# Head transposes on TensorE instead of the DMA crossbar, low fp16 halves also on GpSimd, gated products 1024 columns wide, and a new order of steps

## The chip, the cores and the metric

The kernel runs on one core of a Trainium2 chip. The metric is the device time of one execution in microseconds. The core has TensorE (PE, matrix products; its weight loads are listed apart as PEld), VectorE (DVE), ScalarE (ACT), GpSimd (POOL) and SyncE (SP), which here only issues DMAs. Sixteen DMA engines serve all queues. PE writes to eight PSUM banks of 128 x 512 fp32 each; GpSimd does not touch PSUM in this kernel.

## What is computed

The reference is a gated linear recurrence with a complex decay, followed by a gated feed-forward network (FFN):

```
mag = sqrt(a_re**2 + a_im**2);  a = (a_re + i a_im) * min(mag, 0.999) / (mag + 1e-6)
for t in range(768):                      # S: 48 x 48, complex, one per batch and head
    S = a[t][:, None] * S + outer(k[t], v[t])
    y[t] = q[t] @ real(S)
x = y, heads joined: 3072 tokens x 384
out = (sigmoid(x @ w_gate) * (x @ w_val)) @ w_out      # 384 -> 1536 -> 384
```

There are 4 batches, 8 heads and 768 time steps; inputs and output are fp32.

## The kernel before

Time is cut into 6 chunks of 128 steps. A **slab** is one chunk of one batch with its 8 heads: 24 slabs, `m = 0..23`, in 8 groups (`SIZES`) of 2 or 4. Two slabs make a **pair**, the unit of the FFN.

For each group the decays become sums over time: `sq` and `add` make the squared magnitude, `lna`, `lnm` take logarithms, `inv`, `r` and `atan` give the angle. From group 2 on (`SPLIT`) a logarithm or angle is split into two fp16 halves, so that its running sum is two fp16 matmuls instead of an fp32 one. The high half is `lh` (logarithm) or `th` (angle, in turns). The low half is `ll` (lines 630 to 633) or `tl` (lines 767 to 770), one DVE instruction each: clamp or scale the fp32 value, subtract the high half. PE then forms the running sums (`cl` at line 662, `ct` at line 783). ACT takes exponentials (`ee`) and, after DVE has found whole turns (`r16`, line 798) and PE has taken them off (`nid`, line 805), cosines and sines (`cs`).

For each slab `qke` multiplies q and k by the exponentials. `qs` (line 851, DVE) multiplies by cosine and sine and writes a `slot`: 128 time steps x 16 blocks of 128 columns, eight for k and eight for q. Scores need these blocks with time along the columns, so all 16 must be transposed. Slabs 0 to 5 do it on PE: a step `tp` for each half of the heads makes 8 transposes into one PSUM bank (lines 892 and 893), and a step `qkT` copies 128x1024 fp16 values to SBUF (line 521 on DVE or 519 on ACT, in the helper `copied`). Slabs 6 to 23 (`CROSSED`) do it with two DMAs each, `xk` and `xq` (line 871), through the crossbar of the DMA engines, issued on SP's queue between the loads, the small row copies (line 678) and the stores.

Then, for each slab: scores (`sc`, line 911, PE), a causal mask (`mst`, line 926, DVE, two of 128x512), the state of the recurrence (`u`, `x16`, `kv`, `P`), the result `y` (lines 984 and 986), its scaling to fp16 (`y16`), a PE transpose (`xp`, line 1018) and a copy (`xt`) into the FFN's input.

The FFN of a pair has 12 blocks of 128 hidden columns, taken two at a time (`fp = 0..5`): `pg` and `pv` (line 1043, 6 matmuls of 128x256 each) write a bank each, `tanh` (line 1054, ACT) reads the gate's bank and writes `g16`, and `p` (line 1061, DVE) computes (tanh + 1) * value into `p`, 128x512 at a time. `po` (line 1082) multiplies by `w_out`, `ot` scales and `st` (line 1104) stores.

The order is written out. `TIMES` gives each step a due time; `Plan.order` sorts all steps by it, `manual_schedule` emits them in that order, and each engine and each DMA queue works through its own steps in that order. `HOME` names the engine of each movable step (v for DVE, a for ACT, g for GpSimd). `SLOTS` gives each step its buffer or PSUM bank, and `WARM` puts dummy matmuls ahead of some PE steps.

Of the kernel before, what the change touches and what calls it, by code (L numbers as in the profile page):

```python
# [10 lines left out]
ALU = mybir.AluOpType  # L11
# [16 lines left out]
CROSSED = range(6, 24)  # L28
# [6 lines left out]
    "sq": "vagvaaggaagagagaaggagggg",  # L35
    "add": "vvvvgggggggggggggggggggg",
    "lh": "gvggggvggggg",
    "r": "vvgggggggggg",
    "v16": "vavagaggggagggggagavaaga",
    "qke": "vvvggggvggggggggggggvggg",  # L40
    "th": "aagvaagvgaav",
    "ab": "vvavvavaavaaaaaaaaaavaaa",
    "qkT": "vavavvvvavvvvvvvvvvvvvvvvvvvvvvvvvvvvvvvvvvvvvvv",
    "P": "vava",
    "u": "ggggggvggggggggggvgg",
    "x16": "ggaavgaggggvggag",
    "y16": "avvvaavvavavvvavaaavaaaa",
    "xt": "vvvvvvavvvvvavvavvvvvaav",
    "ot": "vvvvvaaavvvvavvaaavvaaavv",
# [4 lines left out]
        27.89, 36.02, 27.27],  # L54
    "wv": [
        31.35, 38.17, 36.03],
    "wo": [
        53.47, 54.3, 65.03],
    "lr": [
        0.75, 2.68, 7.03, 7.06, 24.34, 27.88, 25.83, 26.32, 45.89, 58.15,  # L60
        53.31, 52.18, 71.46, 92.9, 87.25, 85.33, 106.38, 121.07, 118.57,
        112.93, 170.37, 176.96, 133.38, 160.02],
    "la": [
        2.22, 1.85, 10.78, 7.07, 24.5, 26.36, 25.84, 27.87, 48.76, 56.39,
        53.93, 53.32, 75.86, 92.85, 87.77, 85.34, 111.4, 121.08, 121.86,
        118.56, 176.57, 178.21, 153.22, 134.91],
    "sq": [
        7.04, 7.02, 11.86, 9.9, 24.95, 29.54, 26.34, 29.5, 49.21, 58.89,
        56.85, 62.71, 83.72, 96.51, 92.96, 86.01, 112.9, 129.56, 128.24,
        118.61, 180.83, 185.55, 167.29, 170.36],  # L70
    "add": [
        7.05, 7.9, 13.4, 13.88, 26.35, 38.15, 28.5, 38.12, 53.3, 65, 62,
        65.86, 87.2, 96.54, 96.47, 92.92, 121.81, 129.58, 128.25, 129.55,
        184.23, 185.57, 169.56, 170.39],
    "lna": [
        9.92, 14.99, 33.31, 67.86, 98.47, 139.01, 185.56, 171.42],
    "lh": [
        8.54, 14.47, 40.53, 42.65, 69.29, 75.89, 102.61, 103.34, 136.22,
        141.84, 185.59, 172.91],
    "lnm": [  # L80
        11.87, 15.39, 38.16, 66.46, 100.65, 132.15, 185.58, 170.4],
    "inv": [
        9.93, 16.37, 36.01, 70.07, 103.36, 139.02, 186.18, 172.85],
    "r": [
        10.77, 19.16, 40.52, 39.65, 73.59, 75.88, 108.19, 107.9, 142.65,
        142.64, 189.11, 173.82],
    "cl": [
        14.97, 14.96, 17.84, 16.27, 45.44, 42.85, 47.17, 46.54, 70.89, 76.95,
        80.11, 77.54, 104.14, 104.52, 114.2, 116.75, 138.97, 140.17, 148.32,
        149.93, 187.16, 186.78, 181.01, 173.23],  # L90
    "ee": [
        16.91, 14.98, 18.49, 17.83, 47.18, 44.65, 48.42, 47.56, 72.96, 79.27,
        86.25, 79.29, 106.53, 106.39, 114.78, 117.62, 140.01, 141.81, 149.19,
        152.85, 189.76, 189.77, 182.5, 173.81],
    "scr": [
        35.3, 38.13, 41.19, 37.26, 52.64, 53.49, 54.34, 53.48, 87.94, 92.86,
        95.76, 92.91, 118.58, 111.43, 121.83, 124.54, 153.21, 155.22, 160.22,
        160.21, 195.89, 195.1, 187.57, 187.58],
    "rbt": [
        46.92, 48.74, 55.48, 96.46, 126.03, 161.47, 198.36, 188.29],  # L100
    "arr": [
        50.09, 50.04, 55.92, 98.24, 127.86, 161.92, 205.03, 188.88],
    "lk": [
        16.93, 15.41, 15.42, 17.85, 30.76, 49.23, 53.94, 66.48, 75.91, 85.35,
        94.86, 88.08, 112.25, 92.84, 112.27, 118.55, 125.19, 156.21, 161.95,
        146.39, 185.54, 190.51, 161.93, 181.02],
    "lq": [
        16.94, 16.28, 16.95, 21.91, 41.18, 50.73, 62.72, 69.68, 79.24, 92.87,
        95.78, 88.09, 112.26, 104.92, 122.21, 118.59, 155.19, 156.9, 161.96,
        146.4, 190.31, 197.73, 161.94, 190.12],  # L110
    "lv": [
        15.4, 29.55, 9.91, 26.79, 30.86, 50.74, 71.28, 66.47, 52.19, 92.94,
        76.96, 95.79, 133.17, 121.82, 125.2, 146.64, 160.01, 154.52, 171.41,
        166.24, 140.93, 180.62, 192.37, 195.11],
    "v16": [
        15.89, 30.3, 14.95, 27.29, 45.52, 60.69, 71.29, 84.58, 87.19, 101.96,
        114.07, 118.91, 136.26, 130.58, 142.92, 147.37, 164.44, 155.21,
        178.63, 169.53, 167.28, 202.72, 198.62, 205.05],
    "qke": [
        17.82, 16.36, 20.04, 24.35, 48.73, 53.28, 67.87, 71.45, 84.59, 93.48,  # L120
        96.49, 92.93, 112.96, 108.55, 134.93, 121.8, 157.53, 160.03, 167.43,
        157.52, 209.72, 205.09, 191.58, 190.32],
    "atan": [
        14.48, 21.92, 40.57, 75.9, 108.2, 143.28, 191.6, 176.95],
    "ct": [
        15.44, 15.43, 22.66, 24.05, 48.2, 49.65, 58.14, 59.2, 83.81, 87.93,
        91.11, 87.21, 116.85, 121.09, 130.19, 122.59, 151.79, 158.27, 164.99,
        155.16, 205.89, 202.2, 191.28, 189.92],
    "r16": [
        15.45, 18.69, 23.57, 25.71, 49.24, 50.7, 58.9, 59.78, 84.57, 89.07,  # L130
        91.94, 87.95, 117.61, 121.2, 132.12, 123.7, 152.84, 159.36, 165.57,
        156.87, 207.37, 204.03, 192.35, 190.49],
    "nid": [
        16.92, 19.28, 24.33, 26.3, 49.49, 52.17, 59.3, 60.37, 85.16, 89.47,
        92.89, 88.87, 118.54, 121.4, 132.33, 124.35, 153.03, 160, 166.46,
        157.5, 208.97, 205.07, 192.97, 191.11],
    "cr": [
        20.92, 23.58, 25.85, 28.76, 50.72, 53.37, 62.74, 64.56, 87.18, 91,
        95.81, 89.85, 119.29, 122.19, 134.27, 126.29, 156.88, 161.48, 167.96,
        157.86],  # L140
    "ab": [
        17.28, 20.91, 26.31, 26.78, 52.62, 53.29, 60.7, 63.2, 87.24, 91.46,
        95.8, 89.46, 118.9, 122.61, 134.26, 126.3, 155.17, 162.17, 167.97,
        158.26, 209.12, 205.47, 195.76, 192.33],
    "cs": [
        21, 23.59, 26.51, 30.73, 52.63, 54.33, 65.04, 65.87, 88.07, 92.06,
        98.25, 91.47, 121.01, 124.52, 134.92, 126.94, 156.89, 162.18, 170.33,
        160.19, 209.71, 205.48, 195.77, 192.34],
    "qs": [
        21.9, 24.04, 29.56, 33.52, 54.31, 56.84, 67.89, 72.97, 89.48, 94.21,  # L150
        98.26, 92.95, 122.6, 125.18, 136.25, 128.26, 157.55, 163.7, 175.58,
        160.2, 210.61, 207.38, 198.38, 192.88],
    "tp": [
        24.94, 24.49, 26.86, 25.82, 30.88, 33.51, 34.4, 34.25, 56.38, 61.19,
        63.19, 59.9],
    "qkT": [
        26.18, 26.33, 27.86, 28.51, 34.86, 34.87, 38.11, 38.14, 59.65, 61.99,
        63.91, 61.2],
    "sc": [
        30.87, 26.8, 29.51, 30.31, 36, 35.29, 39.63, 38.75, 63.38, 62.7,  # L160
        64.55, 65.43, 76.51, 76.73, 80.49, 79.88, 99.76, 98.23, 103.88,
        103.37, 108.76, 108.54, 110.29, 105.52, 133.14, 130.57, 133.37,
        132.11, 144.9, 144.91, 141.57, 146.38, 167.92, 166.23, 170.32, 170.09,
        182.04, 182.27, 179.73, 179.08, 219.4, 218.3, 218.53, 215.46, 205.46,
        204.01, 202.19, 202.47],
    "mst": [
        30.89, 27.26, 31.34, 30.74, 37.25, 35.55, 40.05, 39.66, 64.58, 63.18,
        64.99, 65.85, 79.26, 77.55, 82.04, 82.03, 102, 99.99, 104.53, 103.57,
        110.54, 110.53, 114.09, 106.37, 133.57, 132.13, 134.9, 133.19, 145.74,
        145.73, 144.93, 148.33, 168.49, 167.42, 171.45, 170.52, 184.25,  # L170
        183.56, 182.51, 181.03, 220.93, 221.67, 220.95, 217.02, 205.91,
        204.43, 204.02, 204.04],
    "kv": [
        30.75, 40.06, 77.33, 35.62, 84.19, 72.09, 98.02, 90.24, 111.38,
        111.17, 121.02, 125.17, 144.87, 141.37, 152.83, 166.03, 180.81,
        171.19, 180.6, 186.17],
    "P": [
        39.64, 45.46, 79.28, 40.54, 87.17, 75.87, 101.65, 90.99, 112.95,
        112.94, 121.1, 127.85, 144.94, 142.63, 153.44, 168.15, 183.57, 186.38,
        181.05, 192.36],  # L180
    "y": [
        31.46, 33.3, 37.89, 42.66, 67.91, 67.88, 87.23, 85.97, 102.59, 105.07,
        116.74, 121.03, 136.85, 137.26, 146.6, 148.7, 171.4, 171.84, 186.37,
        183.14, 221.99, 221.25, 207.36, 205.1],
    "y16": [
        34.24, 34.88, 38.76, 42.68, 69.67, 69.27, 88.11, 86.71, 103.55,
        105.77, 116.76, 121.13, 138.98, 139, 148.73, 149.96, 172.01, 172.45,
        187.59, 187.81, 222.6, 222.41, 207.97, 205.88],
    "xp": [
        34.85, 35.83, 41.17, 44.62, 71.27, 70.08, 88.7, 87.76, 104.91, 106.36,  # L190
# [971 lines left out]
```

## Time and profile before

| | |
|---|---|
| median of 3 runs | 247.29 us (247.19 to 247.33) |
| profiled execution | 246.99 us |
| its span in the profile | 244.9 us |
| busy: PE, DVE, ACT, POOL | 215.4, 206.3, 198.6, 145.9 us |
| granted PE clock | 1.00 in every stage |
| DMA | 41.75 MB, mean 170 GB/s |
| SP's queue, crossbar transposes | 36, median 1285 ns of issue each |

An engine's busy time is the time in which at least one of its instructions ran. Instructions of one engine overlap a little, so that the sum of the durations is above the busy time. The costliest groups of part 5 give line, engine, operation, tiles and count, then busy time, mean duration in ns, and the idle time just before them.

### The profile page before, as it was taken

Reading aid. Unit: us, or ns where it says so; the run is one execution under the profiler, and the core shown is the slowest. Engines: PE = TensorE matmul, PEld = TensorE weight load, DVE = VectorE, ACT = ScalarE, POOL = GpSimd, SP = SyncE. Lnnn points to the kernel's source line nnn. Section 1 sums busy time; section 2 is a strip of 40 time slices with the busy share of each in tenths; the row PEclk is TensorE's granted clock in tenths of the full one; section 3 lists DMA queues with packets and bytes.
Section 4 is the critical chain, followed back from the end, with each engine's and each line's share of the span. In section 5 each row is a group of like instructions: output and inputs, shape, how many; then the busy total and the mean of one; then the engine's idle time right before and its main releaser. Section 6 shows DMA issues by size and latency. Waiting matters only on the chain.

```text
span 244.9 us, 6068 instructions
## 1 busy us (share of the span) xinstructions
PE 215.4 (88%) x2319; PEld 168.5 (69%) x2319; DVE 206.3 (84%) x317; ACT 198.6 (81%) x326; POOL 145.9 (60%) x138
## 2 busy tenths in 40 slices
PE   0376899959787997999999999999999999999993
PEld 0234688738556865778867778877788777788981
DVE  4589999999888999999999979989887977988250
ACT  2899899948599989999989999996899995542341
POOL 2305977895567899758659986499776683100000
PEclk9999999999999999999999999999999999999999
DMA  7999999999999999999999998979999569073011
GB/s 144 215 218 212 197 183 192 177 191 175 177 180 137 202 244 186 196 177 219 197 192 205 195 212 172 220 165 178 196 191 205 131 136 197 35 141 98 3 64 66
DMA packets 171004, 41.75 MB, mean 170 GB/s; under 512 B 163916, under 2 KB 170976, under 8 KB 170976
## 3 DMA queue, kind: packets, MB, share of 16 engines
q1 hardware_dynamic: 166800, 37.80, 78.3%
q0 software_dynamic: 4176, 3.57, 9.6%
q8 instruction: 18, 0.29, 0.5%
q14 instruction: 10, 0.08, 0.1%
HBM read 30.67 MB, written 4.72 MB: 145 GB/s over the span
## 4 chain that ended last, share of the span: by engine, by line
PE 50%; DVE 15%; ACT 13%; SPq 8%; DMA 8%; issue 4%; DVEq 0%; ACTq 0%
PE banks L1043 25%; PE banks L1082 15%; SPq L552 7%; DMA qk<-in_q_dram 5%; DVE a L768 3%; DVE slot L851 3%; PE banks L911 2%; DVE p L1061 2%; ACT g L1054 2%; DMA qk<-in_k_dram 2%; PE banks L783 2%; DMA a<-in_a_im_dram 1%; DVE qk L728 1%; DVE r L798 1%; ACT lm L604 1%
## 5 line engine op out<-in xcount | busy, mean ns | idle before, releaser
L1061 DVE SCALAR_TENSOR_TENSOR p<-g,banks 128x512 f16<-128x512 f16 x72 | 47.7, 681 | 12.5 <-ACT g L1054 7.4
L1043 PE MATMUL banks<-xt,wg 128*128 128x256 f16 x432 | 56.0, 273 | 0.7 <-DVE xt L521 0.4
L1043 PE MATMUL banks<-xt,wv 128*128 128x256 f16 x432 | 56.2, 273 | 0.0
L1082 PE MATMUL banks<-wo,p 128*128 128x384 f16 (+1 forms) x300 | 55.5, 320 | 0.5 <-ACT g L1054 0.3
L1054 ACT ACTIVATE g<-banks 128x512 f16<-128x512 f32 x72 | 41.2, 601 | 16.8 <-PE banks L1043 11.6
L1043 PEld LDWEIGHTS <-wg 128*128 128x128 f16 x432 | 40.9, 98 | 7.8 <-issue 1.5
L1043 PEld LDWEIGHTS <-wv 128*128 128x128 f16 x432 | 41.4, 98 | 6.8 <-issue 0.5
L728 POOL TENSOR_TENSOR qk<-qk,ee 128x768 f32<-128x768 f32 x19 | 35.3, 1863 | 14.5 <-ACT cr L815 6.8
L851 DVE TENSOR_TENSOR slot<-qk,banks 128x1536 f16<-128x1536 f32 x24 | 41.8, 1745 | 1.7 <-issue 1.3
L1082 PEld LDWEIGHTS <-p 128*128 128x128 f16 x300 | 27.7, 97 | 14.6 <-issue 1.6
L1125 ACT ACT_TABLE_LOAD x28 | 35.9, 1283 | 0.5
L926 DVE TENSOR_TENSOR mst<-banks,msk_t 128x512 f16<-128x512 f32 x48 | 31.9, 685 | 3.4 <-PE banks L911 2.9
L647 POOL TENSOR_TENSOR a<-a 128x768 f32<-128x768 f32 x10 | 18.7, 1884 | 10.7 <-ACT a L641 8.6
L591 POOL TENSOR_TENSOR lm<-sq 128x384 f32<-128x384 f32 x20 | 21.2, 1064 | 4.2 <-ACT sq L583 3.8
L585 POOL TENSOR_TENSOR sq<-a 128x768 f32<-128x768 f32 x12 | 18.2, 1513 | 6.2 <-DMA a<-in_a_im_dram 4.3
L911 PEld LDWEIGHTS <-qkT 128*128 128x128 f16 x192 | 13.2, 97 | 3.2 <-DVE qkT L521 1.1
L940 POOL TENSOR_TENSOR state<-state,arr 128x384 f32<-128x384 f32 x15 | 12.5, 837 | 4.2 <-DVE arr L697 3.4
L583 ACT ACTIVATE sq<-a 128x768 f32<-128x768 f32 x10 | 8.6, 856 | 7.9 <-DMA a<-in_a_re_dram 7.8
L658 PE MATMUL banks<-lm,wl_t 128*128 128x384 f32 x8 | 4.6, 700 | 10.9 <-ACT lm L604 10.9
L768 DVE SCALAR_TENSOR_TENSOR a<-a 128x768 f16<-128x768 f32 x10 | 13.8, 1409 | 0.0
L798 DVE TENSOR_SCALAR r<-banks 128x384 f16<-128x384 f32 x24 | 13.2, 549 | 0.6 <-PE banks L783 0.4
L815 ACT ACTIVATE cr<-banks 32x384 f32<-32x384 f32 x20 | 9.7, 484 | 4.7 <-PE banks L805 4.0
(93 smaller groups left out, 411.8 us busy)
## 6 DMA issues: line engine op xcount, KB each, us to landing
a<-in_a_re_dram SPq DMA_DIRECT2D x24, 192.0 KB
a<-in_a_im_dram SPq DMA_DIRECT2D x24, 192.0 KB
v<-in_v_dram SPq DMA_DIRECT2D x24, 192.0 KB
qk<-in_k_dram SPq DMA_DIRECT2D x24, 192.0 KB
qk<-in_q_dram SPq DMA_DIRECT2D x24, 192.0 KB
out_dram<-ot SPq DMA_DIRECT2D x23, 192.0 KB
wg<-in_moe_w_gate_dram POOLq DMA_DIRECT2D x3, 384.0 KB, 7.7
wv<-in_moe_w_val_dram POOLq DMA_DIRECT2D x3, 384.0 KB, 10.6
```

Of the source, the lines that this page charges most:

```text
L585: on.tensor_tensor(out=T[SQ], in0=T[A][:, :, s], in1=T[A][:, :, s], op=ALU.mult)
L591: home("add", m).tensor_tensor(out=T[LM][:, s], in0=T[SQ][:, 0], in1=T[SQ][:, 1], op=ALU.add)
L647: home("r", w).tensor_tensor(out=T[A][:, 1, i:j], in0=T[A][:, 1, i:j], in1=T[A][:, 0, i:j], op=ALU.mult)
L728: home("qke", m).tensor_tensor(out=T[QK], in0=T[QK], in1=T[EE], op=ALU.mult)
L768: nc.vector.scalar_tensor_tensor(out=turns(T)[:, i:j, 1], in0=T[A][:, 1, i:j], scalar=1.0 / TWO_PI, op0=ALU.mult, in1=turns(T)[:, i:j, 0], ...
L851: nc.vector.tensor_tensor(out=T[SL].rearrange("p i h (r x) -> p r i h x", r=2)[:, :, :, :, 0:D], in0=T[QK].rearrange("p i (h d) -> p i h d ...
L926: nc.vector.tensor_tensor(out=T[MS][:, :n_], in0=T[SC], in1=msk_t.unsqueeze(1).broadcast_to([L, n_, L]), op=ALU.mult)
L1043: nc.tensor.matmul(T[ACC][:, r], wt[:, j, f0:f0 + 128], T[XT][:, :, j], start=(j == 0), stop=(j == 2))
L1054: nc.scalar.activation(out=T[G16], in_=T[PG], func=FT.Tanh, scale=0.5)
L1061: nc.vector.scalar_tensor_tensor(out=T[PT][:, 2 * fp:2 * fp + 2], in0=T[G16], scalar=1.0, op0=ALU.add, in1=T[PV], op1=ALU.mult)
L1082: nc.tensor.matmul(T[PO][:, :wd], T[PT][:, fb, s0:s0 + L], wo16[:, fb, c0:c0 + wd], start=(fb == 0), stop=(fb == NFB - 1))
L1125: nc.scalar.preload_act_table_set(SETS[key[1]])
```

## The change

Six things change.

1. `CROSSED` is empty: all 24 slabs transpose on PE. SP issues 36 DMAs fewer; PE has 48 `tp` steps instead of 12 (384 slot transposes instead of 96) and there are 48 `qkT` copies instead of 12 (41 on DVE and 7 on ACT, where it was 9 and 3).
2. The low halves `ll` and `tl` can be put on GpSimd, as two instructions through a rewritten fp32 tile. `HOME` puts 4 of 10 `ll` and 6 of 10 `tl` there.
3. The value product `pv` of two neighbouring `fp` goes into two neighbouring PSUM banks, and `p` reads both: 36 instructions of 128x1024 instead of 72 of 128x512. `tanh` stays at 128x512, two of them write one `g16` tile of 4 blocks. `g16` has 2 buffers instead of 3. The two `pv` banks come free only after the wide `p`.
4. `TIMES`, and with them the order on every engine and queue, are new; so are `SLOTS`.
5. `HOME` moves other steps between engines too.
6. `WARM` has 93 dummy matmuls instead of 131.

Table loads on ACT become 32 instead of 29. The core of the diff:

```diff
-CROSSED = range(6, 24)
+CROSSED = ()
...
-    "r": "vvgggggggggg",
-    "v16": "vavagaggggagggggagavaaga",
-    "qke": "vvvggggvggggggggggggvggg",
-    "th": "aagvaagvgaav",
-    "ab": "vvavvavaavaaaaaaaaaavaaa",
-    "qkT": "vavavvvvavvvvvvvvvvvvvvvvvvvvvvvvvvvvvvvvvvvvvvv",
+    "r": "vvvvgvgggggg",
+    "v16": "gvvaggggaaggaggaggvaagvg",
+    "qke": "gvgggvgggggggggggggggvgg",
+    "th": "aagvaagggvvg",
+    "ab": "vvaaavaavavvvaavaaavaava",
+    "qkT": "vvvvvvvvvvvvvvvvvvvvvvvvavvvvvvvvavavvaaavvvavvv",
...
+    "ll": "vvvvvvgvvggg",
+    "tl": "vvvgvggvvggg",
...
-    t_g16 = kind("g16", 3, [L, 2, PAIR * L], F16)
+    t_g16 = kind("g16", 2, [L, 4, PAIR * L], F16)
...
+                if home("ll", w) is nc.gpsimd:
+                    nc.gpsimd.tensor_scalar(
+                        out=T[LM][:, i:j], in0=T[LM][:, i:j], scalar1=LNCAP,
+                        scalar2=-200.0, op0=ALU.min, op1=ALU.max)
+                    nc.gpsimd.tensor_tensor(
+                        out=T[LH][:, 1, i:j], in0=T[LM][:, i:j],
+                        in1=T[LH][:, 0, i:j], op=ALU.subtract)
+                    return
...
+                if home("tl", w) is nc.gpsimd:
+                    scaled(nc.gpsimd, T[A][:, 1, i:j], T[A][:, 1, i:j],
+                           1.0 / TWO_PI)
+                    nc.gpsimd.tensor_tensor(
+                        out=turns(T)[:, i:j, 1], in0=T[A][:, 1, i:j],
+                        in1=turns(T)[:, i:j, 0], op=ALU.subtract)
+                    return
...
-                PG, PV, G16 = (bank("g", w, fp, cut=PAIR * L),
-                               bank("v", w, fp, cut=PAIR * L), t_g16(w, fp))
+                r2 = fp % 2
+                PG = bank("g", w, fp, cut=PAIR * L)
+                if not r2:
+                    PV, G16 = bank("v", w, fp, wide=2), t_g16(w, fp)
...
+                if not r2:
+                    continue
...
                     nc.vector.scalar_tensor_tensor(
-                        out=T[PT][:, 2 * fp:2 * fp + 2], in0=T[G16],
-                        scalar=1.0, op0=ALU.add, in1=T[PV], op1=ALU.mult)
+                        out=T[PT][:, 2 * fp - 2:2 * fp + 2].rearrange(
+                            "p i x -> p (i x)"),
+                        in0=T[G16].rearrange("p i x -> p (i x)"),
+                        scalar=1.0, op0=ALU.add,
+                        in1=T[PV].rearrange("p r x -> p (r x)"), op1=ALU.mult)
...
-                            after=ps[2 * i:2 * i + 2] + [ou_keys[i]]
+                            after=[ps[i], ou_keys[i]]
```

## The prediction

> **What bounds the kernel now.** I read, in order, the page's busy shares and slices, the stages of the run, the chain of work that ended last, and single rows.
>
> The page, parts 1 and 2:
>
> ```profile
> PE 215.4 (88%) x2319; PEld 168.5 (69%) x2319; DVE 206.3 (84%) x317; ACT 198.6 (81%) x326; POOL 145.9 (60%) x138
> ...
> PE   0376899959787997999999999999999999999993
> ...
> DVE  4589999999888999999999979989887977988250
> ```
>
> No share is near 100%, but the slices differ: VectorE is full first, PE from about the sixteenth slice on. So I look for the point where the limit changes hands. The attention work of the first twelve slabs (half of them) reaches the FFN with the last of their copies into `xt`; in the trace these are two DVE copies:
>
> ```profile
> 127.05 0.60 DVE L521 COPY xt<-banks 128x384 f16<-128x384 f16 x2
> ```
>
> So the cut is at 127.65 us. The stages on both sides of it (length, then busy time of PE, PEld, DVE, ACT, POOL):
>
> ```profile
> 0.00:20.00 20.00, 7.79 (x37) 4.58 (x38) 12.90 (x30) 14.47 (x21) 4.64 (x12) 1.00 0.97 193
> 20.00:120.00 100.00, 87.14 (x1017) 69.00 (x1014) 94.89 (x137) 90.04 (x142) 76.20 (x67) 1.00 1.08 189
> 120.00:127.65 7.65, 7.27 (x85) 5.02 (x83) 7.65 (x14) 6.99 (x14) 5.28 (x5) 1.00 1.00 210
> 127.65:241.00 113.35, 113.24 (x1190) 89.92 (x1189) 90.82 (x139) 86.62 (x151) 59.78 (x56) 1.00 0.71 149
> ```
>
> Behind the cut PE is idle for 0.11 us in 113. Ahead of it DVE is busy 94.89 of 100 us, PE only 87.14, and the DMA engines are full (share 1.00 to 1.08). The end of the chain agrees: from 128 us on it is nearly all PE, and it closes with
>
> ```profile
> 237.04 3.91 PE banks L1082 x24
> 240.97 0.49 ACT ot L512
> ```
>
> So span = (time at which DVE has pushed twelve slabs through) + (PE work queued behind that) + 3.9 us for the last output copy and store. The profiled execution took 246.99 us, 2.09 more than its span of 244.9; the median of the runs is 247.29, 0.3 above it. I work from 246.99.
>
> **Durations.** Engines overlap neighbouring instructions, so I take start-to-start times where instructions stand back to back.
>
> ```profile
> 25.28 0.22 PE L892 MATMUL banks<-idn_t,slot 128*128 128x128 f16 x1
> 25.34 0.22 PE L893 MATMUL banks<-idn_t,slot 128*128 128x128 f16 x1
> 25.39 0.22 PE L892 MATMUL banks<-idn_t,slot 128*128 128x128 f16 x1
> ...
> 68.37 0.68 DVE L521 COPY qkT<-banks 128x1024 f16<-128x1024 f16 x1
> 68.96 1.30 DVE L926 TENSOR_TENSOR mst<-banks,msk_t 128x512 f16<-128x512 f32 x2
> ```
>
> A PE transpose lasts 0.22 but costs 0.0555, so a step of eight costs 0.445 us; a `qkT` copy costs 0.60 (68.37 to 68.96) against its 0.68. In the same way every DVE cost below is about 0.08 under its mean duration: `p` 0.60, 384-wide copies 0.47, `qs` 1.66. On PE, a `pg` or `pv` step costs 0.655 (the chain's 72 matmuls in 7.86), a `po` step 0.65 (24 in 3.91).
>
> **The change, part by part.** The counts come from the order of instructions of the two kernels.
>
> *Crossbar out.* 36 transposes leave SP's queue, each 1.285 us of issue there, in front of the loads queued behind them. In return PE gets 288 transposes (36 steps x 0.445 = 16.0 us), DVE 32 and ACT 4 more `qkT` copies (32 x 0.60 = 19.2 us on DVE). 38 warm-up matmuls go (2.1 us). PE's total rises by 13.9 us.
>
> The Trainium skill, "VectorE: DVE Perf Modes", section "The three transpose paths", puts a 128x128 transpose at 390 ns on TensorE and 1309 ns on the crossbar. The trace's 0.0555 us is seven times below that TensorE figure, which is a latency and not a rate when many stand in a row; with 390 ns as a cost the 288 would add an estimated 112 us, so the row decides.
>
> *Wide `p`.* The trace has no 1024-column one. By the rows 128x512 (681 ns) and 128x1536 (1745 ns, line 851) an element costs 1.04 ns, so it lasts about 1.21 and costs about 1.13 us. The bounds are 1.20 (two of today's, nothing saved) and 1.07 (the fixed part quite gone). I take 1.13, from the slope: 36 x (1.20 - 1.13) = 2.5 us less in all. A wide `p` waits for two `tanh` and two `pv` steps. Next behind it in DVE's queue stand 9 times a `qkT` copy, 5 times a mask and 5 times a state addition, and scores, `y` and `kv` on PE wait for those. Today's 72 waited 11.8 us in all on ACT and PE (7.4 + 4.4); half as many instructions could wait for half of it or for all of it again, between -5.9 and +5.9, mostly behind the cut, where DVE has 22 us of slack. I take 0.
>
> *Low halves on GpSimd.* Four `ll` and six `tl` leave DVE; a `tl` today:
>
> ```profile
> L768 DVE SCALAR_TENSOR_TENSOR a<-a x10: 949/1247/2555, 47.8 to 205.8; 128x768 f16<-128x768 f32 x10
> ```
>
> Mean 1.41, cost 1.38; `ll` costs 0.87. On GpSimd the two operations are 0.83 (the rows of 128x768 with one input) + 1.81 (two inputs, line 647's median) = 2.64 us. With the shifts of other steps between engines GpSimd's total grows by some 23 us, ahead of the cut by about 9.6. It is idle there for 15.4 + 23.8 + 2.4 = 41.6 us, which hides it unless its steps become links of the chain (below).
>
> The same 128x768 instruction takes from 949 to 2555 ns. The Trainium skill, "SBUF — State Buffer", section "Who interferes with whom", says that a DVE instruction with two SBUF inputs and a GpSimd instruction that reads SBUF lock each other out. That fits the spread; it speaks for taking `tl` off DVE and against giving GpSimd two instructions in its place.
>
> *New order, ahead of the cut.* The cut in the new order is the copy of slab 9 (on ACT), again the last of twelve. Difference in DVE's queue ahead of it: `qkT` +17 (10.2 us), `qs` +2 (3.3), `r` +3 (2.6), `lh` +2 (1.45), `r16` +2 and `P` +2 (1.9), `ab` and `arr` +1 each (0.8); `tl` -3 (4.1), `qke` -2 (2.5), `p` 30 narrow to 14 wide (18.0 to 15.8, 2.2), `ot` -4 (1.9), `add` -2 (1.0), `ll` -1 (0.9), `xt` -3 (0.8), `th` -1 (0.6), and `u`, `x16`, `y16` -1 each (1.2). Sum: 20.25 - 15.2 = **+5.0 us**. ACT's queue ahead grows by about as much (two table loads at 1.283, `ot` +4, `xt` +3), but ACT is idle there for 16.2 us. PE has 16 more transpose steps ahead, in its own gaps of 25 us.
>
> *Behind the cut.* `tp` +20 (8.9), `pv` +2 (1.3), `po` -2 (1.3), `ct` -2 (0.65), `nid`, `kv`, `rbt` -1 each (0.45): **+7.8 us**. Nothing hides it, because PE is full there.
>
> *New waits.* Each transpose step hands over to a copy and each copy to scores. In the list of waits the twelve present steps cost PE 2.5 us (1.1 and 0.5 for scores waiting on DVE's `qkT`, 0.9 for a transpose behind ACT's), 0.21 each. The 20 added behind the cut could cost 0 (FFN work stands between) to 4.2 us; I take the middle, **+2.1**, as these twelve ran early, where PE had less to fill in. The gain side (loads sooner) is the second rival.
>
> Sum: 5.0 + 7.8 + 2.1 = 14.9, so 246.99 + 14.9 = **261.9 us**. PE's total alone (+13.9, idle time unchanged) gives 260.9.
>
> **Rivals.**
> 1. *GpSimd becomes a link.* `th`/`tl` and `lh`/`ll` stand in series before the prefix matmuls; four such pairs ahead of the cut lengthen their chains by 1.69 (`ll`, 2.64 - 0.95) and 3 x 1.23 (`tl`), 5.4 us together, and may block a DVE instruction for up to 1.6 us each (2555 - 949), 6.4 us. All of it: 261.9 + 11.8 = 273.7. For: the waits of GpSimd on ACT's group steps. Against: its 41.6 idle microseconds.
> 2. *Loads come sooner, in part.* The DMA share is at or over 1.0 up to the cut and the chain has stretches on loads behind transposes (112.6 to 119.8 us). Without crossbar the 5.1 us in which DVE is idle between 20 and 120 us go, perhaps the new waits too: 254.7 to 256.8.
> 3. *Faster.* Freed DMA engines would have to take all of DVE's idle time ahead of the cut, 7.1 + 5.1 = 12.2 us, and the port waits of `tl` and `qke` left there (about 2.3), with no new wait: 246.99 + 12.8 - 14.5 = 245.3. It decides once the last of twelve copies ends before 119.4 us (127.65 - 7.8 - 0.5). Against it: 7.1 of that idle time lie in the first 20 us, where no transposes run, and the load of PE behind the cut stays.
>
> **Chances.** My sum (257 to 267) 0.64, rival 1 0.13, rival 2 0.15, no difference within 0.2% (about what a measurement of this kernel can tell) 0.03, rival 3 0.05. So faster 0.05, same 0.03, slower 0.92. The range runs from rival 2's low end to waits of 4.2 with 6.4 us of blocking: 246.99 + 12.8 + 4.2 + 6.4 = 270.4, so 255 to 270; it leaves out the faster and equal cases and about half of rival 1.
>
> **What would show it.** Right: the last of the first twelve `xt` copies ends near 133 us; PE then runs about 120 us almost without a gap; 36 `p` of some 1.21 us; 41 DVE `qkT` copies at 0.68; DMA share clearly under 1. Wrong: a copy before 128 us (loads had been the limit); PE gaps of several us behind it (waits mis-sized); or idle DVE ahead of the cut, released by GpSimd.

## The result, and the profile after

| | before | after |
|---|---|---|
| median, all runs beside each other | 247.31 us (247.19 to 248.78, 4 runs) | 260.99 us (260.09 to 261.87, 4 runs) |
| profiled execution, its span | 246.99, 244.9 us | 261.87, 260.1 us |
| busy PE, DVE, ACT, POOL | 215.4, 206.3, 198.6, 145.9 | 231.1, 212.1, 209.3, 165.3 |

The ratio is 1.054 (95% interval 1.048 to 1.060): slower. The forecast was 261.9, with a range of 255 to 270. The profiled execution, from which the sum was made, grew by 14.88 us (forecast 14.9); it is the slowest of the four, and the medians are 13.7 us apart. The medians of the experiments leave out five executions that took over 1.5% longer than the fastest of their kernel, among them the profiled one of `a_tp_twice_behind`, whose granted PE clock was 0.67 almost throughout and whose cut is therefore not given.

The page of the changed kernel, parts 1 and 2:

```profile
PE 231.1 (89%) x2569; PEld 184.6 (71%) x2569; DVE 212.1 (82%) x300; ACT 209.3 (80%) x338; POOL 165.3 (64%) x156
...
PE   1448869778699999999999999899999999999994
...
DVE  4876999998879999898999878988967878978351
...
PEclk9995999999999999999999999999999999999998
DMA  7999999699998742665859593341960013010011
```

PE is full from about the twelfth slice (72 us) on. The DMA row differs most from before: from the thirteenth slice on the DMA engines have room. The clock row shows a 5 that was not there.

Now the cut of the prediction, the end of the last `xt` copy of the first twelve slabs, and the stages on both sides of it (length, then busy PE, PEld, DVE, ACT, POOL):

```profile
133.72 0.49 ACT L514 ACTIVATE xt<-banks 128x384 f16<-128x384 f16 x1 [0.34 <-PE banks L1028]
```

```profile
0.00:20.00 20.00, 7.33 (x22) 3.63 (x22) 12.47 (x27) 14.53 (x19) 8.83 (x14) 0.99 0.98 192
20.00:120.00 100.00, 88.42 (x1052) 71.03 (x1052) 91.70 (x129) 92.25 (x147) 75.95 (x73) 0.97 0.85 157
120.00:134.21 14.21, 14.21 (x160) 11.41 (x159) 12.75 (x19) 12.59 (x25) 11.99 (x11) 1.00 0.85 180
134.21:256.20 121.99, 121.05 (x1342) 98.55 (x1339) 95.21 (x127) 89.44 (x150) 68.53 (x61) 1.00 0.35 81
```

The cut moved from 127.65 to 134.21 us (+6.6) and the stretch behind it from 113.35 to 121.99 (+8.6); the last copy and store take 3.9 us as before. Together that is the 15.2 us by which the span grew. Behind the cut PE's busy time rose from 113.24 to 121.05 us, +7.81, and its idle time from 0.11 to 0.94. Ahead of it DVE's busy time rose only from 115.44 to 116.92 us, while its idle time rose from 12.2 to 17.3.

Where that idle time comes from is in the waits. DVE, 20 to 134.2 us of the changed kernel (total, times, longest):

```profile
DVE slot L861 <- ACT banks L850: 2.8, 2, 2.0
DVE qkT L516 <- PE banks L903: 2.0, 3, 1.3
DVE mst L936 <- PE banks L921: 1.6, 2, 1.4
DVE banks L840 <- PE banks L815: 1.2, 2, 0.9
```

The same stretch of the kernel before has 0.9 us for `qkT` and 0.5 for `mst`, and neither of the others. The hand-overs between engines, which the prediction priced behind the cut, show ahead of it as idle time of DVE.

PE's rows give a second reading of the later cut. First two stretches of the changed kernel, then one of the kernel before:

```profile
80.00:100.00 20.00, 19.21 (x227) 15.52 (x227) 19.27 (x28) 19.76 (x33) 18.66 (x16) 1.00 0.57 121
100.00:120.00 20.00, 19.90 (x258) 16.46 (x256) 18.90 (x29) 17.90 (x33) 15.70 (x17) 1.00 0.50 102
```

```profile
100.00:120.00 20.00, 19.92 (x235) 16.38 (x232) 19.57 (x34) 19.67 (x27) 14.12 (x14) 1.00 1.09 192
```

In the changed kernel PE is idle for only 0.9 us between 80 us and the cut, and 23.4 of its 24.25 us of idle time ahead of the cut lie before 80 us. In the kernel before, PE is idle for 0.46 us of the last 27.65 us ahead of the cut, where DVE is nearly full too (19.57 of 20 us in the row shown). So in both kernels PE is full well ahead of the cut, which is not the point at which the limit passes to it. Over the whole stretch ahead of the cut PE's busy time rose from 102.20 to 109.96 us (+7.8), and its idle time fell from 25.45 to 24.25.

The operations that the trace of before did not have, from the queries on their lines:

```profile
L1084 DVE SCALAR_TENSOR_TENSOR p<-g,banks x36: 1202/1220/1222, 45.0 to 252.5; 128x1024 f16<-128x1024 f16 x36
```

```profile
L774 POOL TENSOR_TENSOR a<-a x6: 1639/1650/2227, 51.1 to 215.9; 128x768 f16<-128x768 f32 x6
```

The wide product lasts 1.22 us (estimate 1.21). GpSimd's subtraction takes 1.65 us (estimate 1.81).

### The profile page after: what moved, and what is told of

The parts are those of the page before. It is cut to its first block, busy times and chain, and to the rows that moved or that the text cites. A ratio compares the mean times of both kernels' runs of the same rounds, so it can differ in the third digit from the quotient of the medians.

```text
span 260.1 us, 6519 instructions
## 1 busy us (share of the span) xinstructions
PE 231.1 (89%) x2569; PEld 184.6 (71%) x2569; DVE 212.1 (82%) x300; ACT 209.3 (80%) x338; POOL 165.3 (64%) x156
## 4 chain that ended last, share of the span: by engine, by line
PE 56%; ACT 12%; DVE 6%; DMA 5%; issue 5%; SPq 2%; POOL 1%; ACTq 0%; DVEq 0%
PE banks L1058 26%; PE banks L1109 14%; PE banks L921 3%; PE banks L902 3%; PE banks L903 2%; ACT L1152 2%; DMA qk<-in_q_dram 2%; ACT g L1072 2%; DMA a<-cr 2%; PE banks L793 2%; DVE p L1084 2%; PE banks L665 1%; DVE slot L861 1%; PE banks L994 1%; PE banks L996 1%
## 5 line engine op out<-in xcount | busy, mean ns | idle before, releaser
L1109 PE MATMUL banks<-wo,p 128*128 128x384 f16 (+1 forms) x300 | 54.8, 319 | 0.0
L1084 DVE SCALAR_TENSOR_TENSOR p<-g,banks 128x1024 f16<-128x1024 f16 x36 | 43.7, 1217 | 11.5 <-PE banks L1058 10.6
L731 POOL TENSOR_TENSOR qk<-qk,ee 128x768 f32<-128x768 f32 x21 | 38.6, 1846 | 11.8 <-ACT ee L675 6.3
L1058 PEld LDWEIGHTS <-wv 128*128 128x128 f16 x432 | 40.8, 98 | 6.0 <-issue 0.6
L516 DVE COPY qkT<-banks 128x1024 f16<-128x1024 f16 x41 | 27.5, 684 | 3.5 <-PE banks L903 3.5
L586 POOL TENSOR_TENSOR lm<-sq 128x384 f32<-128x384 f32 x21 | 22.3, 1072 | 9.9 <-DVE sq L580 5.0
L902 PE MATMUL banks<-idn_t,slot 128*128 128x128 f16 x192 | 26.3, 221 | 0.7 <-DVE qkT L516 0.4
L903 PE MATMUL banks<-idn_t,slot 128*128 128x128 f16 x192 | 26.3, 221 | 0.0
L903 PEld LDWEIGHTS <-slot 128*128 128x128 f16 x192 | 18.9, 99 | 1.9 <-issue 1.1
L921 PE MATMUL banks<-qkT 128*128 128x128 f16 x192 | 17.6, 219 | 2.7 <-DVE qkT L516 2.2
L902 PEld LDWEIGHTS <-slot 128*128 128x128 f16 x192 | 18.8, 99 | 1.4 <-issue 0.6
L950 POOL TENSOR_TENSOR state<-state,arr 128x384 f32<-128x384 f32 x16 | 13.6, 860 | 7.3 <-DVE arr L700 7.1
L580 POOL TENSOR_TENSOR sq<-a 128x768 f32<-128x768 f32 x10 | 14.9, 1493 | 3.1 <-DMA a<-in_a_im_dram 2.9
```

The lines of the kernel that those rows point to most:

```text
L516: on.tensor_copy(out=dst, in_=src)
L731: home("qke", m).tensor_tensor(out=T[QK], in0=T[QK], in1=T[EE], op=ALU.mult)
L902: nc.tensor.transpose(tp[:, 4 + i], T[SL][:, 1, h], idn_t)
L903: nc.tensor.transpose(tp[:, i], T[SL][:, 0, h], idn_t)
L921: nc.tensor.matmul(sc[:, 4 * hf * both + i], kt, qt, start=True, stop=True)
L1058: nc.tensor.matmul(acc[:, r], wt[:, j, f0:f0 + 128], T[XT][:, :, j], start=(j == 0), stop=(j == 2))
```

## The experiments

Two theories stood against each other for most of them: mine (DVE's work sets the time of the cut, PE's queue the time behind it), and rivals in which the freed DMA engines, GpSimd, or the waits between engines set it. "Cut" is the same point in each kernel's own profile; "rest" is the span less that. Each ratio is to runs of the kernel before that were made beside that kernel (medians 246.7 to 247.4 us).

| kernel | median us | ratio to before (95%) | cut | rest |
|---|---|---|---|---|
| before | 247.31 | | 127.65 | 117.25 |
| after | 260.99 | 1.054 (1.048 to 1.060) | 134.21 | 125.9 |
| `b_no_crossbar` | 247.72 | 1.001 (0.999 to 1.004) | 128.5 | 117.7 |
| `b_pe_transposes` | 282.69 | 1.147 (1.141 to 1.154) | 139.4 | 141.3 |
| `b_low_on_gpsimd` | 252.13 | 1.023 (1.018 to 1.028) | 128.1 | 121.7 |
| `a_tp_twice_behind` | 268.76 | 1.088 (1.081 to 1.096) | | |
| `a_tp_twice_ahead` | 266.07 | 1.079 (1.072 to 1.086) | 139.2 | 126.4 |
| `a_copy_twice_ahead` | 270.76 | 1.099 (1.088 to 1.109) | 141.4 | 127.4 |
| `a_copy_twice_behind` | 265.95 | 1.075 (1.066 to 1.084) | 134.9 | 129.7 |
| `a_low_on_dve` | 267.51 | 1.085 (1.078 to 1.092) | 139.9 | 127.2 |
| `a_p_in_two` | 261.07 | 1.056 (1.049 to 1.064) | 133.8 | 125.5 |
| `a_new_banks` | 278.35 | 1.125 (1.118 to 1.132) | 144.6 | 133.4 |
| `a_tp_near` | 290.94 | 1.176 (1.169 to 1.184) | 142.3 | 146.4 |
| `a_narrow_p` | 288.12 | 1.166 (1.160 to 1.173) | 142.1 | 142.6 |

### What the crossbar's DMAs had cost

```diff
-            QT = [t_qkT(m, 0), t_qkT(m, 1)]
-            if by_dma:
...
+            QT = [still, still] if by_dma else [t_qkT(m, 0), t_qkT(m, 1)]
```

> The kernel before without its 36 crossbar transposes and with nothing in their place: the scores of slabs 6 to 23, and the products with the carried state, read one constant tile of zeros (this leaves those slabs' results out; every other instruction and the order stay). It prices what the crossbar's DMAs cost the loads beside them. Theory (DVE and PE set the time, the full DMA engines are only busy): 0 to -2 us, near 246. Rival (loads come sooner without it): -5 us or more, 242 or under.

The stages around its cut:

```profile
20.00:120.00 100.00, 89.11 (x1004) 69.63 (x1002) 91.28 (x134) 90.01 (x142) 76.78 (x66) 0.97 0.86 159
120.00:128.50 8.50, 7.92 (x92) 5.77 (x92) 8.50 (x16) 7.04 (x14) 6.15 (x6) 1.00 1.00 216
128.50:242.30 113.80, 113.41 (x1190) 90.00 (x1189) 90.98 (x139) 87.10 (x152) 57.96 (x56) 1.00 0.40 91
```

The DMA share between 20 and 120 us falls from 1.08 to 0.86, and little else moves: the cut lies at 128.5 instead of 127.65, the time is within the noise (interval -0.1% to +0.4%). In this order the 0.22 of DMA share that the crossbar had added was free, and so were the waits for its transposes, which this kernel leaves out too. Rivals 2 and 3 of the prediction, which lived on it, fall.

### PE's and DVE's work, ahead of the cut and behind it

The first pair makes the eight transposes of a step twice, the second makes DVE's copy twice, each for slabs 6 to 13 (ahead) or 14 to 23 (behind):

```diff
-                        for i in range(4):
+                        for i in (*range(4), *range(4 if m in range(14, 24) else 0)):
```

```diff
                         copied(home("qkT", n), T[QT], T[TP])
+                        if n // 2 in range(6, 14) and HOME["qkT"][n] == "v":
+                            nc.vector.tensor_copy(out=T[QT], in_=T[TP])
```

> The changed kernel, with the eight transposes of each step made twice into the same bank for slabs 14 to 23, the 20 steps behind the twelfth slab. Theory (PE's queue sets the time there): 20 x 8 x 0.0555 = +8.9 us. Rival (waits set it, and PE has room): +0 to +3.

> The same for slabs 6 to 13, the 16 added steps ahead of that point: 16 x 0.445 = 7.1 us of PE work. Theory (DVE sets the pace there, PE has gaps of some 20 us): +0 to +2. Rival (PE or its waits set the pace there too, as DVE is idle for 17 us): +4 to +7.

> The changed kernel, with each qkT copy on DVE made twice for slabs 6 to 13: 15 more copies, 15 x 0.60 = 9.0 us of DVE work, nearly all ahead of the twelfth slab. Theory (DVE's work sets the time of that point): +8 to +9. Rival (waits set it, DVE's 17 idle us take the copies): +0 to +4.

> The same for slabs 14 to 23: 14 more copies on DVE, 8.4 us. Theory (PE sets the time there, DVE is idle for 27 of 122 us): +0 to +2. Rival (the hand-over from transpose to copy to score is on the path everywhere): +4 to +8.

Behind the cut, 8.9 us of PE work cost 7.8 us (268.76 against 260.99): PE's queue sets the time there, as predicted. Ahead of it, 9.0 us of DVE work cost 7.2 us at the cut and 9.8 in the median, but 7.1 us of PE work cost 5.0 us at the cut too, where I had expected 0 to 2. The cuts of these two:

```profile
140.87 0.49 ACT L514 ACTIVATE xt<-banks 128x384 f16<-128x384 f16 x1 [0.34 <-PE banks L1030]
```

```profile
138.75 0.49 ACT L514 ACTIVATE xt<-banks 128x384 f16<-128x384 f16 x1 [1.23 <-PE banks L1028]
```

So PE's idle time ahead of the cut (24 us) was not room for these steps: nearly all of it lies before 80 us, and about three quarters of the doubled transposes run behind that, where PE is full. DVE's work still counts: with the copies made twice PE is idle for 34.7 us of the whole run instead of 29.0. Each engine is a link, and work on either is paid at 70 to 80% at the cut. The copies behind the cut cost 5.0 us for 8.4 of work, 3.8 of them behind the cut, between the two expectations: DVE's 27 us of idle time there hide only half.

### The low halves on GpSimd

```diff
-    "ll": "vvvvvvgvvggg",
-    "tl": "vvvgvggvvggg",
+    "ll": "vvvvvvvvvvvv",
+    "tl": "vvvvvvvvvvvv",
```

> The changed kernel with part 2 undone: all ll and tl on DVE in one operation. Theory: three tl and one ll come back into DVE's queue ahead of the twelfth slab, 3.7 to 5.1 us, so 265 to 266. Rival (GpSimd had become a link): the prefix sums start 1.2 to 1.7 us sooner for each step, so under 260. Second rival: DVE has 17 us of idle time there and takes them without loss, so no difference.

`b_low_on_gpsimd` adds the changed kernel's two code blocks and its two `HOME` rows to the kernel before, and keeps its order.

> The kernel before, with part 2 alone: 4 of 10 ll and 6 of 10 tl on GpSimd in two operations, order unchanged. Theory: three tl and one ll leave DVE's queue ahead of the twelfth slab, 3 x 1.38 + 0.87 = 5.0 us, and GpSimd hides its 2.64 us each, so about -5 us, near 242. Rival (GpSimd becomes a link): the longer series th, tl, prefix sum costs 1.2 to 1.7 us per step and eats the gain, so 246 to 252.

The two go opposite ways. In the new order, undoing the part costs 6.5 us, 5.7 of them at the cut (theory: 3.7 to 5.1). One line of DVE shows a reason why it is more than the work that was counted:

```profile
L634 DVE SCALAR_TENSOR_TENSOR lh<-lm,lh 128x768 f16<-128x768 f32 x10 | 14.2, 1428 | 0.2 <-POOL lh L617 0.2
```

The same ten `ll` took 952 ns on average in the kernel before. The Trainium skill, "SBUF — State Buffer", section "Who interferes with whom", says that a DVE instruction with two SBUF inputs, which `ll` is, contends with a GpSimd instruction that reads SBUF. The trace agrees as far as durations and times show it: two of the ten that took 1.58 us, at 80.51 and 109.21 us, began while a GpSimd instruction on `state` was running.

In the old order the part alone costs 5 us (252.13), as the rival had it (GpSimd as a link, 246 to 252). DVE's busy time falls from 206.3 to 198.2 us, ahead of the cut from 115.4 to 112.1, and still the cut does not come earlier (128.1); 4.5 us come behind it:

```profile
128.10:245.90 117.80, 114.20 (x1189) 90.14 (x1189) 86.07 (x133) 86.37 (x150) 73.06 (x68) 1.00 0.70 140
```

PE, idle for 0.11 us there before, is idle for 3.6. Its waits name GpSimd's two subtractions for 1.2 us of that and the crossbar's transposes for 1.5, so that GpSimd as a link is shown for a part only. And DVE's work alone did not set the cut of the kernel before: with 3.3 us less of it PE's idle time ahead of the cut stayed the same (25.0 us against 25.45). The same part is worth 6.5 us in the new order and costs 5 us in the old one; which of the other differences decides that, no run tells.

### The wide products

```diff
+                    for r in range(2):
+                        nc.vector.scalar_tensor_tensor(
+                            out=T[PT][:, 2 * fp - 2 + 2 * r:2 * fp + 2 * r],
+                            in0=T[G16][:, 2 * r:2 * r + 2], scalar=1.0,
...
```

> The changed kernel, with each wide product made as two instructions of 512 columns at the same place, from the same two banks; nothing else moves. The prediction's term: 36 x (1.20 - 1.13) = 2.5 us more on DVE, 14 of 36 ahead of the twelfth slab, so +0.5 to +2.5, near 262.5. Rival (what made the narrow version with early products 27 us slower is the number of instructions): +10 or more.

> The changed kernel with part 3 undone: 72 gated products of 512 columns, pv banks one by one, four g16 buffers of half the size, PSUM banks assigned anew. By the prediction's term 36 x (1.20 - 1.13) = 2.5 us more DVE work in all, about 1.0 us of it ahead of the twelfth slab, so +0 to +2.5, near 262. Rival (the wide product holds two banks and makes PE or ACT wait): narrower products free banks sooner, so 2 us or more faster.

Made in two at the same place, the products cost 3.6 us more of DVE's busy time (215.8 against 212.1; forecast 2.5) and no time that can be measured (261.07 against 260.99, intervals overlapping). `a_narrow_p` also undoes the shared `g16` and the bank pairs, moves half of the products to an earlier place in DVE's queue, and had banks and other buffers assigned anew: +27 us. The waits of its products, over the whole span:

```profile
  PE banks L998: 25.1, 21
  ACT g L1009: 9.0, 10
```

In the changed kernel the first of these waits is 10.6 us. DVE stands in front of products whose inputs are not there, with everything else queued behind. So it is not the width; the next two kernels show what it can be. What the bank pairs and the shared `g16` are worth by themselves was not tried.

### The order and the banks

`a_new_banks` is the changed kernel with another `SLOTS["ps"]` alone. `a_tp_near` moves the `tp` and `qkT` of slabs 6 to 23 in `TIMES` to about 1.3 us of plan ahead of their scores; the moved steps have new banks and buffers in part, all others keep theirs. `b_pe_transposes` is the kernel before with `CROSSED = ()`, its `tp` and `qkT` put in shortly ahead of the scores (some five PE steps between), and banks and other buffers assigned anew.

> The changed kernel in its own order, with only the PSUM banks assigned anew (305 of 353 entries differ, free banks taken by longest release): the control for the two kernels whose banks had to be assigned anew. If the time does not change (within 2 us), their losses come from the place of the moved steps. If banks matter (a step waits for the reader of the bank's last content), +5 to +20 us.

> The changed kernel, with the transposes of slabs 6 to 23 moved down in the queues to about two steps ahead of their scores (before: some eleven PE steps between), other banks unchanged. Theory (the hand-over transpose, copy, score is hidden by the FFN steps between, which the new order provides): +8 to +20 us, the loss that part 1 alone showed beyond its work. Rival (work alone counts, and the loss there came from elsewhere): 0 to +3.

> The kernel before, with part 1 alone: every slab transposes on PE, 36 transpose steps and 36 copies put into its own order shortly ahead of their scores. Theory (DVE sets the pace up to the twelfth slab, PE's queue behind it): 24 of the new transpose steps stand behind that point, 24 x 0.445 = 10.7 us on PE, and 12 slabs' worth of copies, 12 x 0.60 = 7.2 us on DVE ahead of it, so about +18 us, near 265, and a few us more where a score stands right behind its copy. Rival (the crossbar's DMA time was a limit): the DMA engines come free, the point comes earlier than 127.65 us, and the time lies at 255 or under.

The same instructions in the same order with other banks cost 17 us. The waits of PE in that kernel, from 20 us on, with the matmuls of line 1052 (`pg`, `pv`), which need only weights and `xt` as input, and of line 915 (scores):

```profile
PE banks L1052 <- DVE mst L930: 4.1, 4, 2.1
PE banks L915 <- DVE xt L510: 2.4, 2, 2.0
```

A gate or value product reads weights and `xt` and writes a bank; it has nothing of the mask's but the bank, whose last reader the mask is. In the changed kernel the same wait is 0.2 us. PE waits in its queue, so all that stands behind it waits too: over the whole run PE is idle for 40.8 us instead of 29.0. The clock is not the reason, for with a mean granted clock of 0.98 in both the two kernels took 278.1 and 260.1 to 261.6 us.

Moving the transposes near their scores costs 30 us, with the work unchanged. Behind its cut:

```profile
DVE qkT L457 <- PE banks L844: 18.6, 14, 3.3
...
ACT qkT L455 <- PE banks L844: 12.7, 6, 4.5
```

The copies now head DVE's and ACT's queues before PE has reached the transposes. In `b_pe_transposes` DVE's wait for the transposes is the longest one (13.7 us behind its cut), and 36 us are lost where the counted work accounts for 18. Its banks and buffers were new as well, so the split of the other 18 us between place and banks stays open; in the changed kernel's order either alone cost about as much or more.

## Why the prediction was right

Point by point, by its own steps.

- **What bounds it: right behind the cut, in part ahead of it.** 8.9 us of added PE work behind the cut cost 7.8. Ahead of it DVE's work counts (7.2 of 9.0 us), but it is not the only term: in the old order 3.3 us less of it brought the cut no earlier, and PE is full from about 80 us on in the changed kernel, from about 100 us on in the kernel before. The prediction had itself read PE as full from about the sixteenth slice (92 us) on, and put the passing of the limit at 127.65.
- **Behind the cut, +7.8 us of PE work: right,** PE's busy time there rose by 7.81.
- **Ahead of the cut, +5.0 us of DVE work: the size was near, the account was not.** The cut came 6.6 us later, but DVE was only 1.5 us busier; it waited 5.1 us longer, for ACT's sines, PE's transposes and the scores. The instructions were counted rightly, but some of those left on DVE became shorter: `tl` took 0.95 us each ahead of the cut (three) where six had taken 1.71, and `qke` 0.95 (two) where four had taken 1.43.
- **"PE has 16 more transpose steps ahead, in its own gaps": wrong.** This put PE's added work ahead at nothing. Doubled, these steps cost 5.0 of 7.1 us at the cut, and PE was 7.8 us busier ahead of it, with 1.2 us less idle time. With that price the rise ahead of the cut needs no large DVE term.
- **New waits, +2.1 us behind the cut: mis-sized.** PE's idle time there grew by 0.8 us. The waits that grew more were DVE's ahead of the cut (5.1 us), which the prediction had not priced.
- **Wide `p`: right in its duration,** 1.22 us each. Its saving came out larger on DVE (3.6 us instead of 2.5) and is worth nothing that can be measured.
- **Low halves: right in sign,** 5.7 us at the cut in this order against 3.7 to 5.1 expected.
- **Rivals 2 and 3 (loads sooner): excluded** by the time itself and, for the old order, by `b_no_crossbar`, though the DMA share of 1.08 and the stretches of the chain on loads had spoken for them.
- **Rival 1 (GpSimd a link): not in the changed kernel,** which is 6.5 us slower with GpSimd relieved; in the old order it is part of what happened.

That the sum came within 0.1 us of the profiled execution is luck: terms too high and too low cancelled, 5.0 + 7.8 + 2.1 forecast, 6.6 + 8.6 measured, and that execution was the slowest of four. The prediction's other sum, PE's total alone with its idle time unchanged (260.9), fits as well and needs fewer terms. Over the whole run PE's busy time rose by 15.7 us (forecast 13.9), its idle time fell from 29.5 to 29.0, and the span rose by 15.2. A part of the 15.7 is the same work at half the clock (last section). That the idle time stayed the same is a finding about this order and no rule.

The weak place of both sums is the waits. The prediction bounded them at 4.2 us by the waits of twelve present steps; kernels with the same work and another order or other banks lost 17 to 30 us. That the new order and banks would keep the hand-overs covered was taken for granted and not derived. No kernel has the new order together with the crossbar, so what the order alone is worth stays open.

## What to carry to other kernels

Find the point at which the limit passes from one engine to another by looking where each engine's idle time lies, stretch by stretch, and not by a point in the flow of data; behind it, count instructions times start-to-start time in the full engine's queue. Ahead of it, a sum of idle time is room for new work only if it lies where the work will run. A DMA share of 1.08 was no limit here. The place of a hand-over and the reader of a PSUM bank's last content can weigh more than all the work that is moved: change one part of a hand-ordered kernel only together with its order.

## What the runs showed of the hardware that was not expected

The granted PE clock, 1.00 throughout in the profiled execution of the kernel before, fell to about 0.5 from 19.5 to 26 us in that of the changed one. A wait of PE of 3.15 us ends at 18.35 us, shortly before; that it is the cause is not shown, for a wait of 8.1 us that ends at 9.9 us has no such dip behind it. The transposes there start 0.106 us apart instead of 0.0555:

```profile
24.74 0.31 PE L903 MATMUL banks<-idn_t,slot 128*128 128x128 f16 x1
24.84 0.31 PE L902 MATMUL banks<-idn_t,slot 128*128 128x128 f16 x1
24.95 0.31 PE L903 MATMUL banks<-idn_t,slot 128*128 128x128 f16 x1
```

The eight of them lose 0.4 us. PE was busy for 5.6 us between 19.5 and 26 us, of which an estimated 2.8 would have been saved at full clock; what the dip costs in the end was not tried. The changed kernel has 38 dummy matmuls fewer, but shorter dips are also in `b_no_crossbar`, which has all 131, so their number is not shown to be the cause. Nor is the change: other executions of the kernel before had mean granted clocks from 0.984 to 1.00.
